# A two-branch attention kernel on one core: 74 score banks on VectorE in place of 62, and a planner with other VectorE durations

## The chip, the core and the metric

The kernel runs on one core of a Trainium2 chip. A core has engines that run side by side, each with its own list of instructions in fixed order: TensorE (PE) multiplies matrices into PSUM, ScalarE (ACT) computes activations such as the exponential, VectorE (DVE) does elementwise work, copies and reductions, GpSimd (POOL) helps, and SyncE (SP) issues DMA transfers. They wait for each other by semaphores. PSUM has eight banks of 128 partitions by 512 fp32 values. The metric is device time in microseconds (us) of one execution; one run with a profile gives a trace of every instruction.

## The reference

Two independent attention branches over sequences of 2048 rows of width 448, in bf16, whose outputs are put side by side:

```python
# A: 16 query heads of width 28, one shared key and value head
q = (x @ wq) -> [H, S, 28];  k = x @ wk;  v = x @ wv
p = softmax(q @ k.T * 28**-0.5)          # full 2048 x 2048 for every head
a = (p @ v) @ wo
# B: 16 heads, each row sees 8 rows, at distances 0, 2, ..., 14 before it
logits = sum_d(q * k[pos - off]) * scale  # masked where pos - off < 0
b = (sum_w softmax(logits) * v[pos - off]) @ wo
out = concatenate([a, b], axis=-1)
```

Branch A needs 16 x 2048 x 2048 exponentials. Cut into banks of 128 keys by 512 queries these are 1024 score banks, and they are the bulk of the work.

## The kernel before

**The planner.** The program is not written in order. `Gen` adds operations with an engine, an estimated duration, the data that they read and write, a priority (lower goes first) and at times a release time `rel`. `Sched.run` (L157 and after) plays these against a clock of its own and so fixes the order of every engine; `resolve` then derives the semaphore waits from the true dependences. The estimates decide the order alone: on the chip each instruction starts when its engine is free and its waits are met. Durations of VectorE come from `t_dve_ps`, `t_dve_1x` and `t_dve_2x` (L376 to L385), or stand as a number at the operation. `LATS` is the delay until another engine sees a result, `OWN` the delay until a dependent operation on the same engine may start. Operations marked `ring` (scores, exponentials, VectorE's copies of score banks) are kept on time: on TensorE and VectorE no other operation is started if it would end after `limit + EPS`, less `MODE` where it is not a tiled matmul (L227):

```python
if limit is not None and not o.ring and not (o.pv and npv > self.NPV) \
        and T + o.dur > limit + self.EPS - (0 if o.tiled else self.MODE):
```

TensorE also gets dummy matmuls on a tile of zeros (L412, L435, L807) where its recent load is low and there is room before the limit, and the scores can be computed with full-height matmuls (L812) in place of row-tiled ones (L815) for the same purpose.

**Branch A.** 16 quads (4 blocks of 512 queries by 4 groups of four heads), each of 64 score banks. Scores go round a ring of five PSUM banks in two slots, of three and of two banks (`SLOTS`, L26). For every slot TensorE writes the scores (L812/L815), ScalarE takes the exponential of the whole slot in one instruction into `expT` (L832), and TensorE multiplies by V into bank 5, four banks at a time (L878). Two slots make a round, 205 rounds in all.

In some rounds the third bank of the three-bank slot is left to VectorE: `offload` (L893) looks in `OFF_AT` for the round's number within the quad. `d_exp` (L902) then copies the bank, scaled, into half of `d_x` (L911), and after every second such bank evaluates the exponential by a polynomial in three operations on 1024 columns (L920, L922, L924) into `dexp`. The bank is free for new scores once VectorE's copy is done. Quad 0 has no such bank, quad 7 six, the others four: 62.

After each quad VectorE transposes and normalises the result (L938 to L947); after four quads TensorE applies wo (L961), and VectorE copies it out (L971). Queries are projected by L751, squared and corrected by L761 to L769; keys and values by L659 to L734, the keys' masked copies `kz` by L679.

**Branch B** runs in the gaps, 16 blocks of 128 rows, block k released from `B0 + BSTEP * k` on: q and k projections (L1002, copies L1007), v (L1017, L1021) through DRAM (SP: L1024, L1026), products on VectorE (L1043), sums by TensorE (L1052), softmax (L1064 to L1084, its exponential on ScalarE at L1078), weighted values (L1097), sums and wo (L1103 to L1113), output (L1115).

**Start.** The first 1024 rows of A's x come on ScalarE's queue and are transposed by TensorE (L693, copies L701/L704); the first part of wq follows on the same queue (L593, L594) and is spread into `wq4` by VectorE (L636). SP loads wk, then transposing loads of x: 8 for A (L607), which wait for the first x, and 16 for B (L612), which wait for nothing.

Of the kernel before, what the change touches and what calls it, by code (L numbers as in the profile page):

```python
# [6 lines left out]
ALU = mybir.AluOpType  # L7
AX = mybir.AxisListType
# [6 lines left out]
DH = 28  # L15
# [20 lines left out]
EL, EP, EQ = -10.141819427815111, -5.83493489876537, 4.836063470359898  # L36
EOFF = 8
A2 = SCALE * 1.4426950408889634
OFF_AT = {q: (0, 2, 5, 7) for q in range(1, 16)}
OFF_AT.update({q: (0, 2, 3, 5, 7, 8) for q in (7,)})  # L40
OFF_AT[15] = (0, 2, 3, 5)
LATE = 2
PSTT = -1.5
# [50 lines left out]

class Sched:
    LAT = 0.13
    LATS = {"pe": 0.12, "act": 0.18, "dve": 0.08}
    MODE = 0.09
    NPV = 3
    WIN = 2.2  # L100
# [2 lines left out]
    FULL = {2: 1500.0, 3: 1200.0}  # L103
    LOW = 900.0
    QKT = 0.315
    EPS = 0.03
    FILL = None
    OWN = 0.06

    def __init__(self):  # L110
        self.ops = []
# [262 lines left out]


def t_dve_ps(n):  # L376
    return 0.15 + 1.04e-3 * n


def t_dve_1x(n):  # L380
    return Lock(0.16 + 1.04e-3 * n)


def t_dve_2x(n):
    return Lock(0.16 + 0.52e-3 * n)  # L385


def t_act(n):
# [11 lines left out]
class Gen:  # L400
# [185 lines left out]
    def loads(self):  # L586
        g, a = self, self.s.add
# [22 lines left out]
        for c in range(NCH):  # L610
            for t in range(4):
                a("sp", 1.3, one(lambda e, c=c, t=t: e.dma_start(  # L612
                    out=g.xT_B[:, t, 512 * c:512 * c + 512], in_=g.B_x[0, 512 * c:512 * c + 512, XB0[t]:XB0[t] + 128],
                    transpose=True)), W=[("xT_B", c, t)], dsem=f"i_xb{c}.{t}", land=4.5, pr=-16 + c)
        a("sp", 1.2, lambda e: [
            e.dma_start(out=g.wqkv[:, 0:3, 0:2 * D], in_=g.B_wqkv[0:384, 0:2 * D].rearrange("(t p) c -> p t c", p=128)),
            e.dma_start(out=g.wqkv[64:128, 3, 0:2 * D], in_=g.B_wqkv[384:448, 0:2 * D]),
# [15 lines left out]
            out=g.wk4[:, :, :].rearrange("p t (j e) -> p t j e", j=4)[:, :, :, 0:DH],  # L633
            in_=g.wk[:, :, :].unsqueeze(2).to_broadcast([128, 4, 4, DH])), R=["wk", "wkz"], W=["wk4"], pr=-7)
        for t in range(4):
            a("dve", Lock(0.3), lambda e, t=t: e.tensor_copy(  # L636
                out=g.wq4[:, t, :, :].rearrange("p k (j e) -> p k j e", j=4)[:, :, :, 0:DH],
                in_=g.wq[:, :, KC * t:KC * t + KC].rearrange("p k (j d) -> p k j d", d=DH)),
              R=[("wq", min(t, 1)), "wqz", ("d_x", 0, 0), ("d_x", 0, 1)], W=[("wq4", t)], pr=-6 if t == 0 else 1.2 + t)
# [5 lines left out]
    def a_head(self):  # L645
        g, a = self, self.s.add
        g.kz_ops = {}
        for i in range(WARM):
            u = Use(f"warm{i}", (3,))
            a("pe", 0.33, lambda e, u=u: e.matmul(g.bank(u.bank), g.warm[:, 0:128], g.warm[:, :], start=True, stop=True),  # L650
              R=["warm"], use=u, pr=-15)
        for c in range(NCH):
            pr = -9 if c == 0 else c
            HB = g.HB if c == 0 else g.LB
            if c < 2:
                g.a_tr(c)
            u = Use(f"K{c}", HB, late=c == 0)
            for kt in range(4):
                a("pe", t_mm(512), lambda e, u=u, c=c, kt=kt: e.matmul(  # L659
                    g.bank(u.bank), g.wk4[:, kt, :], g.xT_A[:, kt, 512 * c:512 * c + 512],  # L660
                    start=kt == 0, stop=kt == 3),
                  R=[("xT", c, kt), "wk4"], W=[u], use=u, pr=pr, rel=8.0 * min(c, 1), dense=512)
            ksq = g.k_sq[:, c % 2, :]
            if c == 0:
                a("act", t_act(512), lambda e, u=u, ksq=ksq: e.activation(ksq, g.bank(u.bank), ACT.Square),
                  R=[u, "d_u"], W=[("k_sq", c % 2)], use=u, pr=-100)
            else:
                kc = g.kT[:, 512 * c:512 * c + 512]
                a("dve", t_dve_ps(512), lambda e, u=u, kc=kc: e.tensor_copy(out=kc, in_=g.bank(u.bank)),
                  R=[u], W=[("kT", c)], use=u, pr=pr)  # L670
                a("dve", t_dve_2x(512), lambda e, ksq=ksq, kc=kc: e.tensor_tensor(out=ksq, in0=kc, in1=kc, op=ALU.mult),
                  R=[("kT", c), "d_u"], W=[("k_sq", c % 2)], pr=pr)
            a("pe", t_mm(512), lambda e, u=u, ksq=ksq: e.matmul(g.bank(u.bank), g.hq[:, 2, :], ksq, start=False, stop=True, skip_group_check=True),
              R=[("k_sq", c % 2), "hq", "d_u"], W=[u], use=u, pr=pr, dense=512)
            kc = g.kT[:, 512 * c:512 * c + 512]
            a("dve", t_dve_ps(512), lambda e, u=u, kc=kc: e.tensor_scalar(  # L676
                out=kc, in0=g.bank(u.bank), scalar1=g.cols[:, 0:1], scalar2=None, op0=ALU.add),
              R=["kadd"], W=[("kT", c)], use=u, pr=pr)
            g.kz_ops[c] = [a("dve", Lock(0.29), lambda e, j=j, c=c, kc=kc: e.tensor_scalar(  # L679
                out=g.kz[:, j, 512 * c:512 * c + 512], in0=kc, scalar1=g.cols[:, 8 + j:9 + j], scalar2=None, op0=ALU.mult),  # L680
                R=["jmask", ("kT", c)], W=[("kz", c)], pr=4 + c) for j in range(4)]
            if c == 0:
                g.a_q(0, first=True)
            g.a_v(c)

    def a_tr(self, c):

        g, a = self, self.s.add
        for kts in ((0,), (1,), (2,), (3,)) if c == 0 else ((0, 1), (2, 3)):
# [7 lines left out]
            for i, kt in enumerate(kts):  # L697
                dst = g.xT_A[:, kt, 512 * c:512 * c + 512]
                src = lambda u=u, i=i: g.psb[:, 1024 * u.bank + 512 * i:1024 * u.bank + 512 * i + 512]
                if c or kt % 2:  # L700
                    a("dve", 0.42, lambda e, src=src, dst=dst: e.tensor_copy(out=dst, in_=src()),  # L701
                      W=[("xT", c, kt)], use=u, pr=-2 if c else -9)
                else:
                    a("act", t_act(512), lambda e, src=src, dst=dst: e.activation(dst, src(), ACT.Copy),  # L704
                      W=[("xT", c, kt)], use=u, pr=-110)

    def a_v(self, c):
# [12 lines left out]
        for b in range(4):  # L720
# [208 lines left out]
    def a_quad_end(self, sc, t, hf=None):  # L929
# [13 lines left out]
        a("dve", 0.25, lambda e: e.reciprocal(out=g.rden[:, t % 2, bs], in_=pt[:, bs, DH]), R=kk("PV"), W=kk("rden"), pr=p0)  # L943
# [126 lines left out]
    def b_soft(self, k2):  # L1070
# [9 lines left out]
        a("dve", t_dve_1x(256), lambda e: e.tensor_reduce(out=g.ssum[:, :, :], in_=ew, axis=AX.X, op=ALU.add),  # L1080
          R=[("e_t", par)], W=["ssum"], pr=pr)
        a("dve", 0.3, lambda e: e.reciprocal(out=mm(g.rs), in_=mm(g.ssum)), R=["ssum"], W=["rs"], pr=pr)
        for b in range(2):
            a("dve", 0.32, lambda e, b=b: e.tensor_tensor(  # L1084
                out=g.a_n[:, par, b], in0=g.e_t[:, par, b],
                in1=g.rs[:, b, :].unsqueeze(1).to_broadcast([128, WIN, H]), op=ALU.mult),
              R=[("e_t", par), "rs"], W=[("a_n", par, b)], pr=pr)
# [74 lines left out]
```

The softmax here doesn't subtract the row's maximum and nothing guards it: scores larger than these inputs give would overflow.

## Time and profile before

| | us |
|---|---|
| median of 9 runs (lowest, highest) | 460.6 (460.11, 462.28) |
| the profiled execution: its time, and its span | 460.11, 458.0 |
| ScalarE busy | 445.3 |
| TensorE busy (matmuls) | 419.8 |
| VectorE busy | 374.1 |
| first exponential of scores starts, last ends | 11.3, 452.3 |

The span runs from the first to the last instruction; the 2.1 us between it and the execution's time are launch and end. A group's line reads: line, engine, operation, output<-input, shapes, number of instructions, then busy time, mean duration in ns, idle time of its engine just before them and what ended it. Instructions of ScalarE and VectorE overlap their neighbours by a little, so that busy times, which count an instant once, are smaller than the durations' sum. A stage line gives the window, its length, and the busy time and count of each engine, then the granted clock of TensorE (1.00 is full), the share of DMA time and the GB/s.

### The profile page before, as it was taken

What the parts mean: (1) busy time and instruction counts of PE and PEld (TensorE: products, weight loads), DVE (VectorE), ACT (ScalarE), POOL (GpSimd) and SP (SyncE); (2) the same over time, 40 slices, a digit from 0 to 9 for tenths busy, and PEclk for the clock granted to TensorE, in tenths of its full rate; (3) what the DMA queues carried; (4) which work ended last, traced back from release to release, by engine and by line L of the source; (5) the groups of instructions that cost most, each with busy time, mean ns of one, the idle gap of its engine ahead of it and who ended that gap; (6) DMA issues with size and microseconds to landing.
All of it is one profiled execution on the core that took longest, in us unless ns stands there. A gap on an engine that the chain in (4) does not pass through costs nothing.

```text
span 458.0 us, 8928 instructions
## 1 busy us (share of the span) xinstructions
PE 419.8 (92%) x3761; PEld 166.2 (36%) x3818; DVE 374.1 (82%) x617; ACT 445.3 (97%) x429; POOL 14.6 (3%) x37
## 2 busy tenths in 40 slices
PE   8999898899999999999899999999888998989884
PEld 4333232323532444223243434424233443424331
DVE  6754878989899896988989889998989887896852
ACT  3999999999999999999999999999999999999995
POOL 8300000000000000000000000000000000000000
PEclk9999999999999999999999999999999999999999
DMA  9982203002301230002030302202002032200001
GB/s 184 244 107 40 64 30 100 1 1 63 119 11 62 82 102 11 1 6 96 1 102 31 110 11 92 93 10 82 31 1 90 26 118 92 92 11 10 11 7 36
DMA packets 39987, 27.30 MB, mean 60 GB/s; under 512 B 15518, under 2 KB 39592, under 8 KB 39948
## 3 DMA queue, kind: packets, MB, share of 16 engines
q1 hardware_dynamic: 37452, 24.06, 18.9%
q0 software_dynamic: 816, 1.53, 1.5%
q10 hardware_dynamic: 1680, 1.13, 1.0%
q8 instruction: 30, 0.49, 0.5%
q14 instruction: 9, 0.07, 0.0%
HBM read 18.06 MB, written 5.52 MB: 51 GB/s over the span
## 4 chain that ended last, share of the span: by engine, by line
ACT 93%; PE 4%; DMA 1%; DVE 1%; ACTq 0%; issue 0%
ACT expT L832 92%; DMA d_x<-in_A_wq_dram 1%; PE ps L1103 1%; PE ps L815 1%; PE ps L812 1%; PE ps L878 1%; ACT e_t L1078 1%; PE ps L961 0%; PE ps L751 0%; PE ps L1052 0%; DVE qT L769 0%; DVE kT L676 0%; PE ps L659 0%; ACTq L593 0%; ACT outA L968 0%
## 5 line engine op out<-in xcount | busy, mean ns | idle before, releaser
L832 ACT ACTIVATE expT<-ps 128x1024 bf16<-128x1024 f32 (+1 forms) x410 | 439.8, 1222 | 1.8 <-PE ps L815 1.7
L815 PE MATMUL ps<-qT,kT 32*128 32x512 bf16 (+1 forms) x859 | 120.8, 373 | 13.1 <-ACT expT L832 9.5
L878 PE MATMUL ps<-expT,v_aug 128*32 128x512 bf16 (+1 forms) x1022 | 95.2, 376 | 0.2 <-ACT expT L832 0.2
L812 PE MATMUL ps<-qT,kz 128*128 128x512 bf16 (+1 forms) x201 | 55.9, 360 | 13.7 <-ACT expT L832 11.6
L815 PEld LDWEIGHTS ps<-qT,kT 32*128 32x128 bf16 x859 | 30.1, 91 | 92.1 <-ACT expT L832 71.4
L911 DVE TENSOR_SCALAR d_x<-ps 128x512 f32<-128x512 f32 x62 | 42.6, 688 | 20.3 <-PE ps L815 19.4
L878 PEld LDWEIGHTS ps<-expT,v_aug 128*32 128x32 bf16 x1022 | 24.5, 93 | 59.8 <-issue 57.2
L1043 DVE TENSOR_TENSOR stage<-qTB,kTB 112x1024 bf16<-112x1024 bf16 x64 | 41.9, 678 | 2.1 <-PE ps L1052 2.1
L1103 PE MATMUL ps<-ident,prod 128*112 128x128 bf16 x512 | 43.5, 224 | 0.1
L1103 PEld LDWEIGHTS ps<-ident,prod 128*112 128x112 bf16 x512 | 34.7, 129 | 16.2 <-issue 12.9
L1097 DVE TENSOR_TENSOR prod<-Vsh,a_n 128x896 bf16<-128x896 bf16 x64 | 37.4, 614 | 2.5 <-PE ps L1103 2.5
L1002 PE MATMUL ps<-xT_B,wqkv 128*128 128x512 bf16 x116 | 37.8, 383 | 1.2 <-issue 1.0
L922 DVE SCALAR_TENSOR_TENSOR d_u<-d_u,d_x 128x1024 f32<-128x1024 f32 x31 | 37.7, 1215 | 0.2
L924 DVE SCALAR_TENSOR_TENSOR dexp<-d_u,d_x 128x1024 int16<-128x1024 f32 x31 | 37.7, 1215 | 0.1
L920 DVE SCALAR_TENSOR_TENSOR d_u<-d_x 128x1024 f32<-128x1024 uint16 x31 | 37.6, 1211 | 0.1
L812 PEld LDWEIGHTS ps<-qT,kz 128*128 128x128 bf16 x229 | 15.0, 97 | 29.5 <-ACT expT L832 27.4
L1052 PEld LDWEIGHTS ps<-ones,stage 112*128 112x128 bf16 x512 | 18.5, 96 | 8.8 <-issue 4.1
L1052 PE MATMUL ps<-ones,stage 112*128 112x4 bf16 x512 | 21.5, 167 | 0.1
L751 PE MATMUL ps<-xT_A,wq 128*128 128x512 bf16 x62 | 19.2, 383 | 0.6 <-DVE qT L769 0.4
L1110 PE MATMUL ps<-wo_B,oT 112*128 112x448 bf16 x64 | 18.5, 357 | 0.3 <-DVE oT L1106 0.2
L938 DVE STREAM_TRANSPOSE PV_T<-ps 128x512 f32<-128x512 f32 (+1 forms) x17 | 11.5, 679 | 8.4 <-PE ps L878 8.3
L961 PE MATMUL ps<-wo,oTn 128*128 128x448 bf16 x64 | 16.8, 356 | 1.5 <-DVE oTn L947 1.4
(105 smaller groups left out, 305.8 us busy)
## 6 DMA issues: line engine op xcount, KB each, us to landing
Vsh<-v_scratch SPq DMA_DIRECT2D x16, 896.0 KB, 4.7
v_scratch<-Vst SPq DMA_DIRECT2D x16, 112.0 KB, 1.7
out_dram<-outB SPq DMA_DIRECT2D x16, 112.0 KB, 1.7
out_dram<-outA SPq DMA_DIRECT2D x15, 112.0 KB, 1.7
stage<-in_A_x_dram ACTq DMA_DIRECT2D x2, 448.0 KB, 4.7
wqkv<-in_B_wqkv_dram SPq DMA_DIRECT2D x1, 672.0 KB, 8.4
wo_B<-in_B_wo_dram POOLq DMA_DIRECT2D x4, 98.0 KB, 5.4
wo<-in_A_wo_dram POOLq DMA_DIRECT2D x4, 98.0 KB, 6.1
```

The lines of the kernel that those rows point to most:

```text
L812: r = e.matmul(g.bank(b0 + i, nq, nq * k), g.kz[:, j, 128 * tb:128 * tb + 128], g.qT[:, sc % 2, t, q0:q0 + nq], start=True, stop=True)
L815: r = e.matmul(g.bank(b0 + i, nq, nq * k), g.kT[32 * j:32 * j + 32, 128 * tb:128 * tb + 128], g.qT[32 * j:32 * j + 32, sc % 2, t, q0:q0 + ...
L832: x = a("act", t_exp(w), lambda e, b0=b0, w=w, n=n: e.activation(g.expT[:, n % ERING, 0:w], g.ps[:, 512 * b0:512 * b0 + w], ACT.Exp, scale ...
L878: x = e.matmul(g.bank(PVBANK, nq, q0, p0=32 * j, p1=32 * j + 32), g.v_aug[:, w, tb, :], src[:, nq * k:nq * k + nq], start=first, stop=last ...
L911: o = a("dve", t_dve_ps(512), lambda e: e.tensor_scalar(out=xx[:, 512 * h:512 * h + 512], in0=g.bank(bank), scalar1=-128.0 * A2, scalar2=1 ...
L920: a("dve", t_dve_1x(1024), lambda e: e.scalar_tensor_tensor(out=u, in0=lo, scalar=EP * F, in1=lo, op0=ALU.add, op1=ALU.mult), R=di, W=["d_ ...
L922: a("dve", t_dve_1x(1024), lambda e: e.scalar_tensor_tensor(out=v, in0=u, scalar=EQ * F * F, in1=lo, op0=ALU.add, op1=ALU.mult), R=["d_u"] ...
L924: a("dve", t_dve_1x(1024), lambda e: e.scalar_tensor_tensor(out=out, in0=v, scalar=EL / F ** 3, in1=xx, op0=ALU.mult, op1=ALU.subtract), R ...
L1002: a("pe", t_mm(512), lambda e, u=u, t=t, kt=kt, w=w: e.matmul(g.bank(u.bank), g.wqkv[:, kt, w * D + KC * t:w * D + KC * t + 128], g.xT_B[: ...
L1043: op = a("dve", t_dve_2x(1024), lambda e, t=t, qv=qv, kv=kv: e.tensor_tensor(out=g.prodT[0:KC, t, :, :], in0=qv, in1=kv, op=ALU.mult), R=R ...
L1052: r = e.matmul(g.bank(u.bank, 128).rearrange("p (h w) -> p h w", w=WIN)[:, 4 * t:4 * t + 4, w], g.prodT[0:KC, t, w, :], g.ones4[:, :], sta ...
L1103: a("pe", 0.056, lambda e, u=u, t=t, w=w: e.matmul(g.bank(u.bank, 128, 128 * t, p1=KC), g.prod2[:, w, KC * t:KC * t + KC], g.ident[:, :], ...
```

## The change

- `OFF_AT`: quads 1, 3, 5, 7, 9, 11 and 13 give six banks to VectorE (rounds 0, 2, 3, 5, 7, 8), the rest four, quad 0 still none: 74 banks.
- The planner's VectorE figures: the fixed part of a duration goes from 0.15 or 0.16 to 0.067 us, several single figures are lowered likewise; `LATS["dve"]` goes from 0.08 to 0.165, `OWN` from 0.06 to 0.02.
- `EPS` goes from 0.03 to -0.04.
- B's transposing loads of x (L612) read `("xst", 0)`, so that they wait for the first x of A as A's do.
- The copies of K and V at the start get priority -2 (where it was higher), and `BSTEP` goes from 23.6 to 23.0.

What the kernel computes, and with which instructions for a given bank, stays as it was.

```diff
-OFF_AT = {q: (0, 2, 5, 7) for q in range(1, 16)}
-OFF_AT.update({q: (0, 2, 3, 5, 7, 8) for q in (7,)})
+SIX = (1, 3, 5, 7, 9, 11, 13)
+OFF_AT = {q: (0, 2, 3, 5, 7, 8) if q in SIX else (0, 2, 5, 7) for q in range(1, 16)}
 OFF_AT[15] = (0, 2, 3, 5)
...
-    LATS = {"pe": 0.12, "act": 0.18, "dve": 0.08}
+    LATS = {"pe": 0.12, "act": 0.18, "dve": 0.165}
...
-    EPS = 0.03
+    EPS = -0.04
     FILL = None
-    OWN = 0.06
+    OWN = 0.02
...
 def t_dve_ps(n):
-    return 0.15 + 1.04e-3 * n
+    return 0.067 + 1.04e-3 * n
 def t_dve_1x(n):
-    return Lock(0.16 + 1.04e-3 * n)
+    return Lock(0.067 + 1.04e-3 * n)
 def t_dve_2x(n):
-    return Lock(0.16 + 0.52e-3 * n)
+    return Lock(0.067 + 0.52e-3 * n)
...
-                    transpose=True)), W=[("xT_B", c, t)], dsem=f"i_xb{c}.{t}", land=4.5, pr=-16 + c)
+                    transpose=True)), R=[("xst", 0)], W=[("xT_B", c, t)], dsem=f"i_xb{c}.{t}", land=4.5, pr=-16 + c)
...
-                  R=[u], W=[("kT", c)], use=u, pr=pr)
+                  R=[u], W=[("kT", c)], use=u, pr=min(pr, -2))
...
-                  R=[("kT", c), "d_u"], W=[("k_sq", c % 2)], pr=pr)
+                  R=[("kT", c), "d_u"], W=[("k_sq", c % 2)], pr=-2)
...
-              R=["kadd"], W=[("kT", c)], use=u, pr=pr)
-            g.kz_ops[c] = [a("dve", Lock(0.29), lambda e, j=j, c=c, kc=kc: e.tensor_scalar(
+              R=["kadd"], W=[("kT", c)], use=u, pr=min(pr, -2))
+            g.kz_ops[c] = [a("dve", Lock(0.265), lambda e, j=j, c=c, kc=kc: e.tensor_scalar(
...
-          R=[("gcol", c), "v_zero"], W=[("v_aug", 0, c)], use=u, pr=pr)
+          R=[("gcol", c), "v_zero"], W=[("v_aug", 0, c)], use=u, pr=-2)
...
-        a("dve", 0.12 + 1.04e-3 * w, lambda e: e.transpose(
+        a("dve", 0.09 + 1.04e-3 * w, lambda e: e.transpose(
...
-    BSTEP = 23.6
+    BSTEP = 23.0
```

The single durations that the cut leaves out: the spread of wq 0.3 to 0.2, copies of transposed x 0.42 to 0.335, the reciprocal after a quad 0.25 to 0.16, and in B's softmax the sum to 0.5, its reciprocal 0.3 to 0.26 and the product 0.32 to 0.2.

More of the change, by code (lines that the diff above doesn't have):

```diff
@@ L635, in loads @@
         for t in range(4):
-            a("dve", Lock(0.3), lambda e, t=t: e.tensor_copy(
+            a("dve", Lock(0.2), lambda e, t=t: e.tensor_copy(
                 out=g.wq4[:, t, :, :].rearrange("p k (j e) -> p k j e", j=4)[:, :, :, 0:DH],
@@ L700, in a_tr @@
                 if c or kt % 2:
-                    a("dve", 0.42, lambda e, src=src, dst=dst: e.tensor_copy(out=dst, in_=src()),
+                    a("dve", 0.335, lambda e, src=src, dst=dst: e.tensor_copy(out=dst, in_=src()),
                       W=[("xT", c, kt)], use=u, pr=-2 if c else -9)
@@ L942, in a_quad_end @@
         pt = g.PV_T[:, t % 2, :].rearrange("p (b e) -> p b e", e=32)
-        a("dve", 0.25, lambda e: e.reciprocal(out=g.rden[:, t % 2, bs], in_=pt[:, bs, DH]), R=kk("PV"), W=kk("rden"), pr=p0)
+        a("dve", 0.16, lambda e: e.reciprocal(out=g.rden[:, t % 2, bs], in_=pt[:, bs, DH]), R=kk("PV"), W=kk("rden"), pr=p0)
         a("dve", t_dve_1x(w), lambda e: e.tensor_tensor(
@@ L1079, in b_soft @@
           R=[("lg2", par, 0), ("lg2", par, 1)], W=[("e_t", par)], pr=-60)
-        a("dve", t_dve_1x(256), lambda e: e.tensor_reduce(out=g.ssum[:, :, :], in_=ew, axis=AX.X, op=ALU.add),
+        a("dve", Lock(0.5), lambda e: e.tensor_reduce(out=g.ssum[:, :, :], in_=ew, axis=AX.X, op=ALU.add),
           R=[("e_t", par)], W=["ssum"], pr=pr)
-        a("dve", 0.3, lambda e: e.reciprocal(out=mm(g.rs), in_=mm(g.ssum)), R=["ssum"], W=["rs"], pr=pr)
+        a("dve", 0.26, lambda e: e.reciprocal(out=mm(g.rs), in_=mm(g.ssum)), R=["ssum"], W=["rs"], pr=pr)
         for b in range(2):
-            a("dve", 0.32, lambda e, b=b: e.tensor_tensor(
+            a("dve", 0.2, lambda e, b=b: e.tensor_tensor(
                 out=g.a_n[:, par, b], in0=g.e_t[:, par, b],
```

## The prediction

> **What bounds the kernel now.** I read the page first, then the chain of waits, then the waits by engine, then the busy time of stages. The first block is from the page: busy shares, the chain that ended last, the groups.
>
> ```profile
> PE 419.8 (92%) x3761; PEld 166.2 (36%) x3818; DVE 374.1 (82%) x617; ACT 445.3 (97%) x429; POOL 14.6 (3%) x37
> ...
> ACT 93%; PE 4%; DMA 1%; DVE 1%; ACTq 0%; issue 0%
> ...
> L832 ACT ACTIVATE expT<-ps 128x1024 bf16<-128x1024 f32 (+1 forms) x410 | 439.8, 1222 | 1.8 <-PE ps L815 1.7
> L911 DVE TENSOR_SCALAR d_x<-ps 128x512 f32<-128x512 f32 x62 | 42.6, 688 | 20.3 <-PE ps L815 19.4
> ```
>
> ScalarE's exponentials are the path: 439.8 us of a 458.0 us span, with 1.8 us of idle. VectorE idles 20.3 us just before its 62 copies of score banks (L911): it arrives early there and waits for TensorE.
>
> Groups of ScalarE and VectorE with shapes kept apart:
>
> ```profile
> L832 ACT ACTIVATE expT<-ps 128x1024 bf16<-128x1024 f32 x266 | 267.6, 1077 | 0.1
> L832 ACT ACTIVATE expT<-ps 128x1536 bf16<-128x1536 f32 x143 | 214.0, 1497 | 1.8 <-PE ps L815 1.7
> ...
> L911 DVE TENSOR_SCALAR d_x<-ps 128x512 f32<-128x512 f32 x62 | 42.6, 688 | 20.3 <-PE ps L815 19.4 <-PE ps L812 0.6
> ...
> L922 DVE SCALAR_TENSOR_TENSOR d_u<-d_u,d_x 128x1024 f32<-128x1024 f32 x31 | 37.7, 1215 | 0.2
> ```
>
> An exponential of three banks takes 1497 ns, of two 1077, but each begins before its forerunner ends: by the start times in the trace an unstalled one follows 1330 ns after a three-bank one and 904 ns after a two-bank one. One bank is therefore worth 1.330 - 0.904 = 0.426 us of ScalarE. Summing what each start lies beyond those two figures gives 6.9 us of real stall over the exponentials, most of it in pieces of 0.03 to 0.4 us that the idle column hides; eight small softmax exponentials cost 0.31 us each besides.
>
> Busy time in three stages: quads 1 to 13 (a quad is 64 score banks, some 27.5 us), the one quad that already has six banks on VectorE (quad 7), and all after quad 13:
>
> ```profile
> 41.10:398.10 357.00, 333.83 (x2942) 130.19 (x2989) 312.78 (x493) 356.92 (x341) 0.00 (x0) 1.00 0.17 56
> ```
> ```profile
> 205.50:232.30 26.80, 24.48 (x34) 1.00 0.15 48
> ```
> ```profile
> 398.10:452.30 54.20, 36.34 (x54) 1.00 0.04 12
> ```
>
> VectorE (third pair of numbers in the first, the only one in the others) idles 44.2 us in quads 1 to 13, 2.3 us in quad 7, 17.9 us after quad 13.
>
> The chain at the start:
>
> ```profile
> 1.92 4.93 DMA d_x<-in_A_wq_dram
> 6.85 0.02 issue
> 6.87 0.29 DVE wq L636
> 7.16 0.05 issue
> 7.21 1.04 PE ps L751 x4
> ```
>
> The first weights of q, on ScalarE's queue, arrive at 6.85, while SP has three transposing loads of x for B under way since 1.93; the first exponential starts at 11.28.
>
> **The change part by part.**
>
> *Twelve more banks on VectorE.* Quads 1, 3, 5, 9, 11, 13 go from four to six: 62 to 74 banks. ScalarE loses 12 x 0.426 = 5.12 us, all on the path; the number of exponentials stays 410. VectorE gains six pairs. Instructions that wait for nothing start 85 ns before their forerunner's end (436 of 616 successions overlap), so a pair costs 2 x 0.604 + 1.127 + 1.131 + 1.133 = 4.60 us by start-to-start times, six of them 27.6 us. This lies beside ScalarE as long as VectorE has room: quads 1 to 13 would hold 312.8 + 27.6 = 340.4 us in about 352 us, 97%, and work of part B can move into the 17.9 us after quad 13 (its last output is copied at 429.3). Without that cover part of the 27.6 us lands on the path. Each more loaded quad also splits one group of four P·V matmuls into two partial ones: six extra of about 0.40 us (a group of four, timeline) on TensorE, 2.4 us, beside 23.2 us of its idle time in these quads. Rounds with an offloaded bank show a stall of 0.056 us, others 0.030 (sums of the start excesses by kind): 12 x 0.026 = 0.3 us on the path.
>
> *The planner's VectorE durations and latencies* (fixed part 0.15 or 0.16 to 0.067; latency to others 0.08 to 0.165; own dependence 0.06 to 0.02; single figures for small operations). They add no instruction, they reorder. The new figures equal the start-to-start rows: 0.067 + 0.532 = 0.60 for 512 columns against 0.604, 1.13 for 1024 against 1.13. The old ones were some 0.09 high each, 617 x 0.09 = 55 us in all: the old plan saw VectorE full, and on the chip it ran ahead of plan, which is why it sits idle before L911. With the new plan that accidental lead is gone, and a late copy of a score bank holds up the next scores and then ScalarE. What speaks against the new figures is a dependent pair, which follows its forerunner's end by 35 ns, 0.12 after the planned end rather than 0.02; between 41 and 398 us there are 23 such successions, 2.3 us of slip over 13 quads. Cost on the path: from 0 (slack takes it) to 74 x 0.15 = 11 us (every copy late by slightly more than the new 0.13 us margin of 0.09 + 0.04). I take 1.0, near the low end, because quad 7 carries six banks at 91% busy with 0.35 us of ScalarE stall where the other quads of 1 to 13 have 0.32 to 0.60.
>
> The Trainium skill, VectorE: DVE Perf Modes, section The DRAIN you can't avoid, says that the next operation doesn't start until the pipeline is empty, though it excepts operations that are not held. Taken bare that would price six pairs by full durations, 6 x (2 x 0.69 + 3 x 1.215) = 30.2 us, and make every new duration of the plan too short; the 85 ns overlaps of this trace contradict it.
>
> *Dense matmuls kept further from scores* (EPS 0.03 to -0.04, for VectorE's other work ahead of a score copy too). Gain: the small stalls behind two-bank exponentials, 4.4 us in 200 gaps against a floor of 0.006 each, leave at most 3.2 us; loss: 410 score groups x 0.07 = 28.7 us of TensorE's room if every one loses it, against 23.2 us of idle and the dummy matmuls (L412, L435: 57 of about 0.2 us, some 11 us), which only fill. I take a gain of 0.8 between a gain of 3.2 and a loss of 3.2 (as much again), since TensorE's stalls before scores are mostly one matmul long.
>
> *B's transposing loads wait for the first x of A.* SP issues nothing between 1.88 and about 4.6 us, then the eight A loads (issued 1.2 us earlier than now), wqkv, then sixteen B loads at 1.3 us or more. Queued behind the wait are all SP loads; B's fourth block of x lands now at 25.4, after the change at about the same; the last B load, now issued at 36.3, slips to about 40, ahead of the v store (L1024) whose value is first used (L1097) at 93. Gain: the q weights take 4.9 us from issue to landing, the wk load issued at 0.80 took 2.7; without the transposes the weights could come up to 1.0 earlier before the copies of x take over as the last input. Between 0.2 later and 1.0 earlier; I take 0.4 earlier.
>
> *The rest*: B released every 23.0 instead of 23.6 us (up to 9 us earlier at the last block), K and V copies at priority -2. No cost: the K and V copies run before 41 us, where VectorE is busy 15.98 of 29.80 us (stage view), so what they overtake has room; if it had none, each would delay another operation by 0.7 us. B's last copy at 429.3 stands 23 us ahead of the last exponential's end, 452.3. Without that cover, B's lag would show one to one. The tail after 452.3 (5.7 us) is unchanged.
>
> Sum against the profiled execution's 460.11: -5.12 + 0.3 + 1.0 - 0.8 - 0.4 = -5.0, so 455.1. That execution was 0.5 below the median of 460.6, so I predict **455.6**.
>
> **The rivals.**
>
> *Slower: VectorE late at the score copies.* The lead that shows as 20.3 us of idle before L911 is spent, and every copy comes late by some mean time x. It decides at 74 x = 5.0, x = 0.07 us; at 0.15 us it gives 460.6 - 5.1 + 11.1 - 0.4 = 466. For: 97% load in quads 1 to 13. Against: quad 7, and only 3 waits of TensorE for L911 now (1.5 us).
>
> *No gain: stalls eat it.* TensorE's lost room pushes dense work so that scores come late in half of the 205 rounds by 0.05 us: 5.1 us, so 460.6. Against: TensorE can drop its dummies.
>
> *Slower clock.* Fewer dummies let the granted clock drop. All 40 slices show 9 and every stage 1.00, so no row prices a drop; if dense matmuls took double time in two slices (23 us), TensorE's 92% would want some 1.8 times that, up to 18 us: 455.6 + 18 = 474. Against: the fill rule is unchanged.
>
> *The loads change nothing* (hidden): 456.0, inside the forecast's range.
>
> **How the numbers follow.** Forecast 0.66 (own range 453.2 to 458.0: stall gain 3.2 and head gain 1.0 in full, or 2.4 of copy lateness more); late VectorE 0.20 (460.5 to 468); no gain 0.09 (458 to 461); clock 0.05. A measurement here tells 0.2%, 0.9 us, from no change. Faster: 0.66 + 0.04 of the no-gain case = 0.70; same 0.06; slower 0.24. The range must take in about half of the late-VectorE case: 453.0 to 462.5, leaving 0.04 below and 0.16 above.
>
> **What would show it.** Right: exponentials of 1024 columns up by 12 to about 278 and of 1536 down to about 131, ScalarE near 435 us, VectorE near 402, idle before L911 well under 20 us; wq copy earlier than 6.87. Wrong: TensorE's scores waiting for d_x for more than 5 us, ScalarE idle before L832 of several us, B's last copy after 450, a clock below 9.

## The result and the profile after

The changed kernel takes 454.45 us (median of 10 runs, 454.43 to 460.4) against 460.75 us for the kernel before beside it (32 runs, 459.91 to 462.45): a ratio of 0.9876, 95% interval 0.9858 to 0.9894. The prediction was 455.6 us. The profiled execution took 454.94 us, 5.17 us less than the profiled execution of before (460.11), with a span of 452.9 us.

From the page of the changed kernel: busy shares, then the groups that answer to those shown of before.

```profile
PE 416.2 (92%) x3764; PEld 166.1 (37%) x3814; DVE 396.5 (88%) x647; ACT 439.8 (97%) x429; POOL 14.4 (3%) x37
...
L832 ACT ACTIVATE expT<-ps 128x1024 bf16<-128x1024 f32 (+1 forms) x410 | 434.1, 1237 | 2.1 <-PE ps L815 1.9
...
L911 DVE TENSOR_SCALAR d_x<-ps 128x512 f32<-128x512 f32 x74 | 50.6, 683 | 9.5 <-PE ps L815 9.3
```

ScalarE is still the path and has lost 5.7 us of exponentials' busy time; VectorE's idle time before its copies of score banks has fallen from 20.3 to 9.5 us, although there are twelve more of them. The same groups with shapes kept apart, and the stage of quads 1 to 13 (before, the window 41.1 to 398.1):

```profile
L832 ACT ACTIVATE expT<-ps 128x1024 bf16<-128x1024 f32 x278 | 280.5, 1104 | 0.1
L832 ACT ACTIVATE expT<-ps 128x1536 bf16<-128x1536 f32 x131 | 199.7, 1525 | 2.0 <-PE ps L815 1.9
```
```profile
41.10:398.10 357.00, 335.88 (x3005) 132.56 (x3044) 338.61 (x530) 356.90 (x347) 0.00 (x0) 1.00 0.18 56
```

Twelve exponentials went from three banks to two, as planned. VectorE is busy 338.61 us of the 357 (312.78 before): its idle time there went from 44.2 to 18.4 us. (In the changed kernel quads 1 to 13 end some five us before the window does; the rest of it is quad 14.)

To read where time goes, I take each profiled execution apart in four pieces: the start of the first exponential; the floor, which is the sum of 1.330 and 0.904 us over the exponentials of three and two banks; the stalls, by which starts of successive exponentials lie further apart than that; and the tail after the last exponential's end. The rest, 3.3 to 4.6 us, is the last exponential, of one bank (0.6 us), and what the small activations in between take. The table has the runs of the next section too; "B's last copy" is the start of the last L1113.

| kernel | median, lowest | span | first exp | floor | stalls | tail | B's last copy |
|---|---|---|---|---|---|---|---|
| before | 460.75, 459.91 | 458.0 | 11.28 | 430.7 | 6.91 | 5.75 | 429.3 |
| changed | 454.45, 454.43 | 452.9 | 11.41 | 425.5 | 6.51 | 5.76 | 422.3 |
| 74 banks, old plan | 477.38, 477.1 | 475.4 | 11.59 | 425.5 | 7.22 | 27.74 | 472.6 |
| 74 banks, new VectorE figures only | 457.33, 457.2 | 455.3 | 12.18 | 425.5 | 8.20 | 5.77 | 425.0 |
| changed, 62 banks | 463.65, 461.05 | 459.0 | 11.12 | 430.7 | 7.63 | 5.76 | 401.5 |
| the same, a later execution | 464.88 (one) | 462.8 | 11.07 | 430.7 | 10.66 | 5.76 | 405.3 |
| changed, old EPS | 457.13, 455.89 | 457.9 | 11.56 | 425.5 | 10.54 | 5.76 | 427.6 |
| changed, old loads | 455.59, 455.39 | 453.3 | 11.83 | 425.5 | 6.51 | 5.76 | 422.7 |
| changed, late copies | 465.80, 463.95 | 461.9 | 11.76 | 425.5 | 14.99 | 5.75 | 431.3 |
| changed, BSTEP 22.9 | 457.58, 455.38 | 453.3 | 10.89 | 425.5 | 7.22 | 5.76 | 416.8 |
| 78 banks | 453.38, 453.10 | 451.3 | 11.63 | 423.8 | 6.42 | 5.76 | 426.1 |
| 80 banks | 453.40, 452.97 | 451.0 | 11.02 | 423.0 | 6.78 | 6.35 | 441.9 |
| 80 banks, other start | 452.91, 452.23 | 450.8 | 11.44 | 423.0 | 7.36 | 5.76 | 425.6 |
| 88 banks | 464.41, 463.87 | 461.8 | 11.23 | 419.6 | 6.93 | 20.60 | 459.0 |

Between before and after, the floor fell by 5.1 us and the stalls by 0.4, while the first exponential came 0.1 later: with 0.2 us more for the small activations in between that is the profiled difference. A difference of up to 0.4 us in the first exponential's start need not be a kernel's doing: the first x of A, issued at 0.81 us in all these traces, lands at 4.50 us in the changed kernel's and as late as 4.90 in others, with the old loads (4.51 to 4.81) as with the new (4.50 to 4.90).

### The profile page after: what moved, and what is told of

Read it like the earlier page. It is cut to its first block, busy times and chain, and to the rows that moved or that the text cites. A ratio compares the mean times of both kernels' runs of the same rounds, so it can differ in the third digit from the quotient of the medians.

```text
span 452.9 us, 8975 instructions
## 1 busy us (share of the span) xinstructions
PE 416.2 (92%) x3764; PEld 166.1 (37%) x3814; DVE 396.5 (88%) x647; ACT 439.8 (97%) x429; POOL 14.4 (3%) x37
## 4 chain that ended last, share of the span: by engine, by line
ACT 91%; PE 5%; DVE 2%; DMA 1%; issue 0%
ACT expT L832 91%; DMA stage<-in_A_x_dram 1%; PE ps L815 1%; PE ps L812 1%; ACT e_t L1078 1%; PE ps L435 0%; PE ps L878 0%; PE ps L693 0%; PE ps L659 0%; PE ps L961 0%; PE ps L1002 0%; DVE kz L679 0%; DVE xT_A L701 0%; PE ps L722 0%; DVE PV_T L938 0%
## 5 line engine op out<-in xcount | busy, mean ns | idle before, releaser
L832 ACT ACTIVATE expT<-ps 128x1024 bf16<-128x1024 f32 (+1 forms) x410 | 434.1, 1237 | 2.1 <-PE ps L815 1.9
L815 PE MATMUL ps<-qT,kT 32*128 32x512 bf16 (+1 forms) x901 | 127.7, 373 | 15.2 <-ACT expT L832 12.4
L815 PEld LDWEIGHTS ps<-qT,kT 32*128 32x128 bf16 x901 | 31.8, 91 | 93.4 <-ACT expT L832 76.5
L911 DVE TENSOR_SCALAR d_x<-ps 128x512 f32<-128x512 f32 x74 | 50.6, 683 | 9.5 <-PE ps L815 9.3
L812 PE MATMUL ps<-qT,kz 128*128 128x512 bf16 (+1 forms) x162 | 44.9, 357 | 11.5 <-ACT expT L832 10.2
L920 DVE SCALAR_TENSOR_TENSOR d_u<-d_x 128x1024 f32<-128x1024 uint16 x37 | 45.0, 1216 | 0.2
L922 DVE SCALAR_TENSOR_TENSOR d_u<-d_u,d_x 128x1024 f32<-128x1024 f32 x37 | 45.0, 1215 | 0.1
L924 DVE SCALAR_TENSOR_TENSOR dexp<-d_u,d_x 128x1024 int16<-128x1024 f32 x37 | 44.9, 1214 | 0.1
L1052 PE MATMUL ps<-ones,stage 112*128 112x4 bf16 x512 | 22.9, 167 | 0.0
L812 PEld LDWEIGHTS ps<-qT,kz 128*128 128x128 bf16 x187 | 12.3, 97 | 22.1 <-ACT expT L832 20.3
L938 DVE STREAM_TRANSPOSE PV_T<-ps 128x512 f32<-128x512 f32 (+1 forms) x17 | 11.5, 678 | 8.7 <-PE ps L878 8.7
L1017 PE MATMUL ps<-wqv,xT_B 128*128 128x448 bf16 x64 | 18.3, 357 | 0.6 <-DVE kTB L1007 0.5
```

The lines of the kernel that those rows point to most:

```text
L812: r = e.matmul(g.bank(b0 + i, nq, nq * k), g.kz[:, j, 128 * tb:128 * tb + 128], g.qT[:, sc % 2, t, q0:q0 + nq], start=True, stop=True)
L815: r = e.matmul(g.bank(b0 + i, nq, nq * k), g.kT[32 * j:32 * j + 32, 128 * tb:128 * tb + 128], g.qT[32 * j:32 * j + 32, sc % 2, t, q0:q0 + ...
L832: x = a("act", t_exp(w), lambda e, b0=b0, w=w, n=n: e.activation(g.expT[:, n % ERING, 0:w], g.ps[:, 512 * b0:512 * b0 + w], ACT.Exp, scale ...
L911: o = a("dve", t_dve_ps(512), lambda e: e.tensor_scalar(out=xx[:, 512 * h:512 * h + 512], in0=g.bank(bank), scalar1=-128.0 * A2, scalar2=1 ...
L920: a("dve", t_dve_1x(1024), lambda e: e.scalar_tensor_tensor(out=u, in0=lo, scalar=EP * F, in1=lo, op0=ALU.add, op1=ALU.mult), R=di, W=["d_ ...
L922: a("dve", t_dve_1x(1024), lambda e: e.scalar_tensor_tensor(out=v, in0=u, scalar=EQ * F * F, in1=lo, op0=ALU.add, op1=ALU.mult), R=["d_u"] ...
```

## The experiments

My theory was that the twelve banks are the gain and the planner's VectorE figures are what lets them fit; its main rival, that VectorE becomes late at the copies of score banks and ScalarE pays.

### The banks without the plan, and the plan without the banks

Only the banks, everything else as before:

```diff
-OFF_AT = {q: (0, 2, 5, 7) for q in range(1, 16)}
-OFF_AT.update({q: (0, 2, 3, 5, 7, 8) for q in (7,)})
+SIX = (1, 3, 5, 7, 9, 11, 13)
+OFF_AT = {q: (0, 2, 3, 5, 7, 8) if q in SIX else (0, 2, 5, 7) for q in range(1, 16)}
```

> The kernel before with the 74 banks and nothing else changed: the planner still takes VectorE's instructions for some 0.09 us too long each. Theory (the planner's new figures are what makes the 12 banks fit): the plan sees VectorE over-full, orders score copies late, and ScalarE waits; half of the 5.1 us or more is lost, 457 to 465 us. Rival (the banks alone are worth 0.426 us each whatever the plan): about 455.5 us.

It took 477.38 us (ratio 1.0362, 1.0349 to 1.0375), 12 us above the range of the theory. Yet ScalarE ends its exponentials at 447.6 us, as in the changed kernel (447.1), with about the same stalls (7.22 against 6.51 us). Three stages of this kernel, the last one after the last exponential:

```profile
41.10:398.10 357.00, 334.72 (x2778) 119.99 (x2775) 318.13 (x476) 356.59 (x345) 0.00 (x0) 1.00 0.14 44
398.10:447.60 49.50, 45.35 (x537) 20.59 (x535) 41.40 (x69) 49.49 (x48) 0.00 (x0) 1.00 0.20 64
447.60:475.40 27.80, 20.00 (x231) 12.66 (x229) 18.82 (x38) 0.99 (x3) 0.00 (x0) 1.00 0.19 63
```

VectorE's copies of score banks over the whole run, and then its groups from 448 us on:

```profile
L911 DVE TENSOR_SCALAR d_x<-ps 128x512 f32<-128x512 f32 x74 | 50.9, 688 | 17.1 <-PE ps L815 14.9 <-PE ps L812 1.6
```
```profile
L1097 DVE TENSOR_TENSOR prod<-Vsh,a_n 128x896 bf16<-128x896 bf16 x12 | 7.0, 617 | 1.5 <-PE ps L1103 1.4
L1106 DVE CAST oT<-ps 112x512 bf16<-112x512 f32 x4 | 2.7, 686 | 1.8 <-PE ps L1103 1.8
L1113 DVE CAST outB<-ps 128x448 bf16<-128x448 f32 x4 | 2.5, 625 | 2.1 <-PE ps L1110 2.0
```

The last four of B's sixteen blocks are finished after ScalarE is done. VectorE was not full: in the window 41.1 to 398.1 it idles 38.9 us (357.00 - 318.13) against 18.4 in the changed kernel. The old plan took each instruction for too long, gave the score copies and polynomials their places, and put B's work, which comes later by priority, where it believed there was room: at the end. The planner's own clock, the times that `Sched.run` gives the operations, says so: for this kernel it has VectorE busy 351.8 us of the same 357, where the chip shows 318.13, and starts VectorE's last operation at 470.4 us; for the changed kernel it says 338.6 us, where the chip shows 338.61, and 443.1. So the old figures don't make the copies late, as I had it (VectorE still waits 17.1 us for scores ahead of them); they push the other branch out of ScalarE's shadow.

The figures of VectorE alone, with the 74 banks and without EPS, block step, priorities and loads:

```diff
-    LATS = {"pe": 0.12, "act": 0.18, "dve": 0.08}
+    LATS = {"pe": 0.12, "act": 0.18, "dve": 0.165}
...
-    OWN = 0.06
+    OWN = 0.02
...
-    return 0.15 + 1.04e-3 * n
+    return 0.067 + 1.04e-3 * n
```

> The kernel before with the 74 banks and the planner's new VectorE durations and latencies, but the old EPS, block step, priorities and loads. Theory (the figures make the banks fit, the rest is small): 454.5 to 456.5 us. Rival (the margin EPS is what makes it hold): above 457 us.

457.33 us, 20 us below the kernel with the banks alone: 0.8 us above what the theory gave, and 0.3 us inside the rival's bound, so that the bounds I wrote don't decide; the pieces of the time do. The tail is back at 5.77 us and B's last copy at 425.0, with the old margin. The step from 477 to 457 is the figures', and the tail of 27.74 us against 5.77 is where it lies. The run changes the durations and the two delays together, and no run separates them; by the planner's own clock it is the durations (with these and the old delays VectorE's last operation starts at 444.0 us, with the old durations and the new delays at 469.9). What is left to the changed kernel, 2.9 us by medians and 2.5 by the profiled executions, is in the first exponential (12.18 against 11.41) and in stalls (8.20 against 6.51).

The other way round, the changed kernel with 62 banks:

```diff
-SIX = (1, 3, 5, 7, 9, 11, 13)
+SIX = (7,)
```

> The changed kernel with 62 banks (quad 7 alone has six). Theory (the gain is the 12 banks, 12 x 0.426 us): 5.1 us above the changed kernel, 459.5 us, near the kernel before. Rival (the new order itself removes stalls): under 458 us.

463.65 us, above both forecasts and above the kernel before (ratio 1.0064, 1.0039 to 1.0089). The rival falls: the new order with 62 banks saves nothing. But my 459.5 was missed as well. In its profiled execution, one of its fastest, the floor is exactly back (430.7) and the stalls are 1.1 us longer than the changed kernel's; that makes 6.1 us of span. The other 2.6 us lie between that execution and the median; the next trace is about them.

### One more trace of the kernel with 62 banks

> The 62-bank version of the changed kernel once more, for one more trace: its median (463.65) lay 2.6 us above its profiled execution (461.06). Theory (the granted clock drops in some executions, early, and late scores then stall ScalarE): where this execution takes 463 us or more, its rows show the clock below 1.00 in a stretch, and the exponentials' stalls lie in that stretch. Rival (the time is lost evenly): the clock stays at 1.00 and the stalls are spread.

This execution took 464.88 us. Stages from its start, first of the earlier execution (461.06 us), then of this one; the columns are the busy times and counts of TensorE, its weight loads, VectorE, ScalarE and GpSimd, then the granted clock:

```profile
11.00:16.00 5.00, 4.51 (x40) 1.98 (x37) 4.63 (x13) 4.88 (x5) 4.13 (x7) 1.00 1.18 203
16.00:20.00 4.00, 4.00 (x35) 1.35 (x34) 2.50 (x8) 3.90 (x5) 0.20 (x1) 1.00 1.21 153
20.00:24.00 4.00, 3.76 (x35) 1.62 (x33) 2.16 (x5) 4.00 (x5) 0.00 (x0) 1.00 1.15 261
```
```profile
11.00:16.00 5.00, 3.09 (x27) 1.35 (x25) 3.55 (x11) 4.62 (x4) 4.13 (x7) 0.96 1.22 148
16.00:20.00 4.00, 4.00 (x20) 1.27 (x19) 2.38 (x6) 1.87 (x3) 0.18 (x1) 0.50 1.06 143
20.00:24.00 4.00, 4.00 (x34) 1.01 (x32) 1.21 (x4) 2.71 (x3) 0.02 (x1) 0.70 1.35 129
```

The program is the same. Here the granted clock falls to 0.50 between 16 and 20 us and is 0.70 in the next four; TensorE is busy throughout and does 20 matmuls in place of 35 in the first of these stages, and ScalarE is busy 1.87 us of 4, then 2.71. Three exponentials wait 1.9, 0.9 and 1.4 us for their scores (they start at 17.46, 19.65 and 21.95 us), 4.2 us together; the two executions differ by 3.8 us.

But the trouble starts before the clock falls. The second part of the q weights, which GpSimd issues at 8.4 us, landed at 12.0 us in the earlier execution and at 14.3 us in this one. VectorE's fixed order has the copy of these weights (L636) ahead of its work on the second block of keys (L669, L671), which TensorE's L673 needs. Again first the earlier execution, then this one, and below them TensorE's busy time and clock in the stretch of the drop:

```profile
12.96 0.27 DVE L636 COPY wq<-d_x 128x448 bf16<-128x448 bf16 x1
13.15 0.68 DVE L669 CAST kT<-ps 128x512 bf16<-128x512 f32 x1
14.46 0.39 PE L673 MATMUL ps<-d_u,hq 128*128 128x512 bf16 x1 [0.30 <-DVE d_u L671]
```
```profile
14.35 0.31 DVE L636 COPY wq<-d_x 128x448 bf16<-128x448 bf16 x1 [1.30 <-DMA d_x<-in_A_wq_dram]
14.58 0.67 DVE L669 CAST kT<-ps 128x512 bf16<-128x512 f32 x1
15.83 0.61 PE L673 MATMUL ps<-d_u,hq 128*128 128x512 bf16 x1 [1.72 <-DVE d_u L671]
```
```profile
15.56:22.38 6.82, 6.55 (x35) 0.50 1.14 144
```

VectorE waits 1.30 us for the weights, TensorE 1.72 us for VectorE, and the clock falls during that wait, at 15.56 us, for 6.82 us. L673 starts 1.37 us later than in the earlier execution, so by my estimate some 1.4 of the 4.2 us are the late load's and the other 2.8 the half clock's. The theory of a clock drop holds for the later stalls of this execution; what comes first is a load that landed 2.4 us later. That TensorE's wait is what brings the clock down was not tried; all traces fit it, as the last section says.

### The margin before scores

```diff
-    EPS = -0.04
+    EPS = 0.03
```

> The changed kernel with EPS at 0.03 again. Theory (the margin takes away small stalls and makes executions alike): 455 to 456.5 us, with a wider spread between executions than the changed kernel's 0.1 us in most. Rival (EPS has no effect on the path): within 0.5 us of 454.4.

457.13 us, 0.6 above the theory's range, with executions from 455.89 to 460.08. The profiled one, 459.96 us, shows the same drop behind the same wait. Its row of the weights' copy, then two stages and the stretch of the drop with TensorE's busy time and the clock:

```profile
14.75 0.28 DVE L636 COPY wq<-d_x 128x448 bf16<-128x448 bf16 x1 [1.15 <-DMA d_x<-in_A_wq_dram]
```
```profile
15.00:20.00 5.00, 3.80 (x19) 0.64 1.15 145
20.00:25.00 5.00, 5.00 (x35) 0.68 1.25 122
16.37:23.20 6.83, 6.83 (x36) 0.50 1.16 123
```

Of its 10.54 us of stalls, 3.92 belong to three exponentials in these ten us; the rest, 6.6, is what the changed kernel has (6.51). So the margin does not take away small stalls between scores, though I had expected it, either in this run or in the comparison of before and after (6.91 and 6.51, with 54 and 56 stalls above 0.03 us). The spread between executions was as expected, but that the margin is its reason is not shown: TensorE waited 1.60 us for the keys because the weights landed at 14.7 us, and the changed kernel has the same copy at the same place of VectorE's order.

### A neighbouring order

```diff
-    BSTEP = 23.0
+    BSTEP = 22.9
```

> The changed kernel with BSTEP 22.9 in place of 23.0: the same work in a slightly different order. It shows how far the time moves by the accident of an order. Theory: within 1 us of 454.4. Rival (the order is finely tuned): 1 to 4 us slower.

457.58 us, from 455.38 to 461.35, although the block step differs by 0.4% and the profiled execution, the fastest, is 0.4 us from the changed kernel's profiled one. So the rival holds for the median, and by the fastest executions (455.38 against 454.43) the theory does. Eight of the changed kernel's ten runs lie between 454.43 and 454.94; this kernel's twelve are strewn over 6 us. The clock is not enough to explain that: the seven executions with a mean clock of 0.999 or 1.000 take from 455.38 to 459.14 us.

### The loads at the start

```diff
-                    transpose=True)), R=[("xst", 0)], W=[("xT_B", c, t)], dsem=f"i_xb{c}.{t}", land=4.5, pr=-16 + c)
+                    transpose=True)), W=[("xT_B", c, t)], dsem=f"i_xb{c}.{t}", land=4.5, pr=-16 + c)
```

> The changed kernel, but B's transposing loads wait for nothing again; all engines but SP keep their order. Theory (the q weights come 0.9 us sooner without these loads, but VectorE and TensorE have something else queued ahead): the weights' copy starts near 6.9 us in place of 5.96, the first exponential moves from 11.4 by 0 to 0.9 us later, time 454.4 to 455.4. Rival (loads don't matter): the copy stays near 6.0 and the time at 454.4.

455.59 us against 454.45, and 455.39 against 454.43 by the fastest executions: about 1 us, at the upper end of the theory's range. Every engine but SP has the same order as in the changed kernel. The chain of waits at the start, first of the changed kernel (where the q weights' copy is no longer in it), then with the old loads:

```profile
0.81 3.69 DMA stage<-in_A_x_dram
4.50 0.05 issue
4.55 1.89 PE ps L693 x16
6.44 0.43 PE ps L650
6.86 0.27 PE ps L751
```
```profile
1.93 4.84 DMA d_x<-in_A_wq_dram
6.77 0.02 issue
6.79 0.33 DVE wq L636
7.12 0.04 issue
7.17 0.39 PE ps L751
```

The weights' copy starts at 6.79 us with the old loads and at 5.96 in the changed kernel; the first exponential at 11.83 and 11.41. With the wait, the first x of A and its transposes are the last input in place of the weights. The rival, that the loads don't matter, falls. How much of the 0.42 us between the two first exponentials is the loads' doing these two traces don't show, for the first x itself took 3.7 us to land in the changed kernel and 4.0 here:

```profile
stage<-in_A_x_dram ACTq DMA_DIRECT2D x1, 448.0 KB, 3.7
```
```profile
stage<-in_A_x_dram ACTq DMA_DIRECT2D x1, 448.0 KB, 4.0
```

In the run of the next section, which has the new loads and x landing after 4.1 us, the first exponential starts at 11.76.

### Late copies

```diff
+        self.scr = sb([128, 128], BF16, "scr")
...
-        o = a("dve", t_dve_ps(512), lambda e: e.tensor_scalar(
+        o = a("dve", t_dve_ps(512), lambda e: (e.tensor_copy(out=g.scr[:, :], in_=g.bank(bank, 128)), e.tensor_scalar(
```

> The changed kernel, each engine in the same order, but ahead of each of the 74 copies of a score bank VectorE copies 128 columns of it into a scratch tile, about 0.2 us that the plan doesn't know. It measures what a late copy costs. Theory (the plan's margin of 0.13 us takes most of it): 0 to 0.1 us for each copy, 455 to 462 us. Rival (each late copy is paid in full): 74 x 0.2 = 15 us, 469.

465.80 us, 3.8 us past the theory's end and 3.2 below the rival's 469. Who waited for these two instructions, in us and times:

```profile
L911 DVE CAST scr<-ps x74: 251/281/293, 42.1 to 438.4; 128x128 bf16<-128x128 f32 x74
...
  PE ps L815: 7.1, 17
  PEld ps L815: 3.3, 6
```

TensorE's scores now wait 7.1 us for VectorE's copies in 17 places, in the changed kernel 0.7 us in two:

```profile
  PEld ps L815: 1.7, 4
  PE ps L815: 0.7, 2
```

The stalls grow by 8.5 us, 0.115 us for each copy that is 0.2 late; by medians it is 11.35 us, 0.15 each. The mechanism of my slower rival is therefore real and dear. The plan's margin takes less than half of 0.2 us. It did not happen, because in the changed kernel the copies are on time.

### More banks

```diff
-SIX = (1, 3, 5, 7, 9, 11, 13)
+SIX = tuple(range(1, 15))
```

> The changed kernel with six banks in each of quads 1 to 14, 88 in all. ScalarE has 14 x 0.426 = 6.0 us less, VectorE 7 x 4.6 = 32 us more, 428 in about 447 us. Theory (VectorE has about 19 us of idle in quads 1 to 13 and 15 us after, so it becomes the bound): ScalarE begins to wait for scores and the time is 454 to 470. Rival (there is room, work moves to the end): 448.5.

464.41 us. ScalarE ends at 441.2 us, 5.9 before the changed kernel, with 6.93 us of stalls: it does not wait for scores. The end belongs to B, as in the kernel with the banks alone, this time because VectorE is really full. Its stages, the last one after the last exponential:

```profile
41.10:398.10 357.00, 336.83 (x2833) 120.33 (x2830) 346.60 (x518) 356.84 (x351) 0.00 (x0) 1.00 0.14 45
398.10:441.20 43.10, 39.91 (x519) 19.93 (x519) 42.40 (x72) 43.09 (x43) 0.00 (x0) 1.00 0.22 71
441.20:461.80 20.60, 15.35 (x165) 9.67 (x164) 13.50 (x28) 0.99 (x3) 0.00 (x0) 0.96 0.27 90
```

VectorE is busy 346.60 of 357 and 42.40 of 43.10 us, and B's last copy starts at 459.0. The time lies in the theory's range, but by another way than it named. Between the two lies room: with 74 banks B's last copy is 25 us ahead of ScalarE's end. So I tried 78 and 80.

```diff
-SIX = (1, 3, 5, 7, 9, 11, 13)
+SIX = (1, 2, 4, 6, 8, 9, 11, 12, 14)
...
-    BSTEP = 23.0
+    BSTEP = 22.6
```

> The changed kernel with 78 banks (six in quads 1, 2, 4, 6, 8, 9, 11, 12, 14) and BSTEP 22.6. With 74 banks B's last copy starts 25 us before the last exponential ends, with 88 it starts 18 us after; each pair moved it by some 5 us. Theory (banks pay until B's end meets ScalarE's): 4 x 0.426 = 1.7 us less, 452.8, plus or minus 1 for the accident of the order and up to 3 for a clock drop at the start. Rival (VectorE is already the bound): 455 or more.

453.38 us (ratio 0.985, 0.983 to 0.9869), 1.1 below the changed kernel where 1.7 was expected; the floor gave its 1.7 (425.5 to 423.8).

```diff
-SIX = (1, 3, 5, 7, 9, 11, 13)
+SIX = (1, 3, 4, 5, 7, 8, 9, 11, 13, 14)
...
-    BSTEP = 23.0
+    BSTEP = 22.6
```

> As with 78 banks, but 80 (six in quads 1, 3, 4, 5, 7, 8, 9, 11, 13, 14). Theory: B's last copy some 15 us later than with 74 banks, still before ScalarE's end: 6 x 0.426 = 2.6 us less than the changed kernel, 451.9. Rival: B's part passes ScalarE's end and the tail grows above 5.8 us, 454 to 460.

453.40 us, between the theory's 451.9 and the rival's 454. The floor fell by 2.5, and the tail grew to 6.35 us: B's last copy starts at 441.9, 2.8 us before the last exponential's end at 444.7. The step to 78 banks was paid; in this order the next one was not.

```diff
-                      W=[("xT", c, kt)], use=u, pr=-2 if c else -9)
+                      W=[("xT", c, kt)], use=u, pr=-2 if c else -9, rel=10.4 if c else 0.0)
```

> 80 banks with BSTEP 23.0, and the four copies of A's second transposed block of x released at 10.4 us in the plan, so that none of them stands before the first keys (L676), as one does in the changed kernel (9.84 to 10.25 us). Theory: the first exponential starts 0.3 us sooner than in the changed kernel, at 11.1, the floor of the exponentials is 2.6 us lower and B's last copy stays ahead of ScalarE's end: 451.8 us, up to 1 us off by the accident of the order. Rival (work moved from the start delays B's projections and the tail grows): 453.5 or more.

This last one has the 80 banks of the run before, BSTEP 23.0 and this edit. 452.91 us (ratio 0.9841, 0.9817 to 0.9865) is the lowest median, 1.5 us below the changed kernel. B's last copy is back at 425.6, so the order alone moved it by 16 us. The first exponential did not come sooner (11.44 against 11.41). VectorE's rows at the start, first of the changed kernel, then of this one, and below them the landing of the first x in this one's chain of waits (in the changed kernel's, shown above, it takes 3.69 us):

```profile
9.17 0.75 DVE L769 TENSOR_SCALAR qT<-ps,cols 128x512 bf16<-128x512 f32 x1 [2.27 <-PE ps L765]
9.84 0.41 DVE L701 COPY xT_A<-ps 128x512 bf16<-128x512 bf16 x1
10.17 0.74 DVE L676 TENSOR_SCALAR kT<-ps,cols 128x512 bf16<-128x512 f32 x1
```
```profile
9.38 0.75 DVE L769 TENSOR_SCALAR qT<-ps,cols 128x512 bf16<-128x512 f32 x1 [2.27 <-PE ps L765]
10.19 0.75 DVE L676 TENSOR_SCALAR kT<-ps,cols 128x512 bf16<-128x512 f32 x1
```
```profile
0.81 3.91 DMA stage<-in_A_x_dram
```

Nothing stands between q and k any more, and k follows q after 0.81 us in place of 1.00: the copy in between did hold k up, by 0.19 us rather than 0.3. That k starts at 10.19 us against 10.17 all the same is because x landed 0.22 us later in this execution, and q with it.

## Why the prediction was right, and where not

The predicted 455.6 us was 1.2 above the measured 454.45. By its terms, in the order of its sum:

- *Banks, 5.12 us.* Floor 430.7 to 425.5: as predicted, and unhidden. The number of two-bank exponentials is 278 as named.
- *Dearer rounds, 0.3 us lost.* Not found. By the prediction's own measure, rounds with an offloaded bank stalled 0.055 us and others 0.026 before; in the changed kernel it is 0.038 and 0.028. The stalls as a whole went down by 0.4.
- *VectorE late, 1.0 us lost.* About nothing: 0.7 us of scores waiting for a copy, in two places, with no more stalls of ScalarE. The value from quad 7 would have been nothing too; I added for the lost lead. The lead is not all lost (9.5 us of idle before the copies), and the copies are no more punctual by the new margin: with the old one in the changed kernel no score matmul waits for a copy, and their weight loads wait 2.0 us against 1.7.
- *VectorE's load.* 97% was forecast for quads 1 to 13; 95% was measured (338.61 of 357.00), and 396.5 us in all in place of 402. Where 436 of 616 successions overlapped before, now 523 of 646 do; the 57 beyond the 30 that the new instructions bring are worth 57 x 0.085 = 4.8 us. By the bare rule of the Trainium skill's VectorE: DVE Perf Modes, section The DRAIN you can't avoid, which excepts operations that are not held, I had estimated a gain of 30.2 us for VectorE; it gained 22.4.
- *The margin, 0.8 us gained.* No run shows a gain in the stalls between scores. The run with the old margin is slower by its clock drops and by 1.5 us in its fastest execution, which stays unassigned.
- *The loads, 0.4 us gained.* The weights' copy came earlier as forecast (5.96 against 6.87 us), but against the kernel before the first exponential starts 0.13 us later (11.41 against 11.28), not sooner: q starts 0.20 earlier (9.17 against 9.37), and the new order puts a copy of x between q and k, so that k follows after 1.00 us in place of 0.67. In the changed order the loads are worth about 1.0 us by the times of the run that undoes them, the upper bound of the prediction.
- *From the profiled execution to the median, 0.5 us added.* Wrong in sign: the changed kernel's profiled execution, 454.94, was one of its slower ones, and most others took 454.44.

On profiled executions the sum said -5.0 and the measurement -5.17: 5.1 of banks and 0.4 of stalls gained, 0.3 lost at the first exponential and the small activations. The banks were right by their mechanism. That everything else came out near nothing, as forecast, is partly luck: the sum had +1.3 and -1.2 us of small terms that cancel, and none of them was found as it was sized. By medians 6.3 us were gained; the other 1.1 us is where the two profiled executions lie, 0.6 below the median of before and 0.5 above that of the changed kernel, and no trace shows what the 454.44 us executions do otherwise. The range that I called my own should by its terms have begun at 452.6 in place of 453.2, with both gains in full.

The rivals: *late copies* did not occur, and the late-copy run prices them at 0.115 to 0.15 us for 0.2 us, so that the break-even of 0.07 us mean lateness, at full price, should have stood at about 0.1. *No gain by TensorE* did not occur: it still has 357.00 - 335.88 = 21 us of idle in quads 1 to 13. *A slower clock* occurs, but not as I priced it: not through fewer dummies over the whole run, but in single executions, for 6.8 us near the start, behind a wait of TensorE, at some 4 us with that wait. What I had only as a half-sentence, that part of VectorE's added work lands on the path without cover, is the mechanism that decides: it lands behind ScalarE as B's last blocks, 22 us in one kernel and 15 in another, while the copies stay punctual.

## What to carry to other kernels

Where a planner sets an engine's order, measure start-to-start times of instructions that wait for nothing and plan with those: 0.09 us too much for each of 600 instructions (with the two delays set beside it) cost 20 us here, without any instruction being slower. When work is moved onto a second engine, look at what that engine does last: ordered by priority, the urgent work stays on time and the low-priority work passes the end of the critical engine, so that the distance between those two ends is the room that is left. And where neighbouring orders differ by 1 to 3 us, a single run of each doesn't rank them. And where a copy that waits for a load stands ahead of urgent work in an engine's fixed order, a late landing of that load is on the path; to put such a copy behind the urgent work was not tried here.

## What the runs showed of the hardware that I had not expected

The granted clock of one and the same program fell to 0.50 for 6.82 us in one execution (15.56 to 22.38 us into the program) and not in another; the two differ by 3.8 us (464.88 against 461.06). Another kernel's execution has 0.50 for 6.83 us from 16.37 us on. In both it falls during or just behind an idle stretch of TensorE, of 1.72 and 1.60 us, that a late load brought. In the twelve other traces its longest idle between 11.5 and 30 us is 0.62 us, and the clock stays at 1.00 there. An idle of 1.18 us in the kernel before, at 75.5 us, is followed by no drop. That the idle time brings the drop is what this suggests, and no experiment shows it.

The mean clocks of executions without a trace go along with it for some kernels: of the 62-bank version's twelve, the seven from 463.64 us on have 0.993 or less and the five below 463 have 0.996 or more; with the old margin the six from 457.13 on have 0.993 or less and the five below have 0.997 or more; the changed kernel's one of 460.40 has 0.993. The clock is not the whole of the spread, though. The changed kernel's profiled execution (454.94, mean 0.997) has 1.00 from 6.85 us until 450.58, when TensorE's last matmul is done, and the same tail as the others, so that its 0.5 us above 454.44 have another reason. With BSTEP 22.9 executions at 0.999 or 1.000 differ by 3.8 us, and of the kernel before, beside these runs, executions at 1.000 took from 460.09 to 462.10. What makes these differ was not found.
